# A two-headed SSM kernel with x's first blocks loaded first, more of B turned on TensorE, transfers issued by ScalarE too, and a new order table

## The chip, the cores and the metric

The kernel runs on one core of one Trainium2 chip. The metric is the device time of one launch, in microseconds (us). Three runs of the kernel before took 195.96, 197.85 and 198.28 us, median 197.85 us. In the profile the engines are PE (TensorE; its weight loads are the row PEld), DVE (VectorE), ACT (ScalarE), POOL (GpSimd) and SP (SyncE, which here only issues DMA transfers). A name such as SPq or ACTq is an engine's own queue of instructions.

## What is computed

Two sequence mixers over S = 2048 steps and D = 640 channels, whose results are put side by side. The first (A) is a complex diagonal recurrence, the second (B) a causal convolution of each channel with a filter of 2048 taps, of a product whose one factor is k filtered by four taps.

```python
# A: h[t] = Lam_bar*h[t-1] + B_bar x[t];  y = 2 Re(C h) + x*Dskip
Lam_bar = jnp.exp(dt * Lam);  B_bar = ((Lam_bar - 1.0) / Lam)[:, None] * Bmat
Bu = jnp.einsum("bld,pd->blp", x + 0j, B_bar)
for t in range(L):
    h = Lam_bar[None, :] * h + Bu[:, t, :]
y = 2.0 * jnp.einsum("blp,dp->bld", hseq, Cmat).real + x * Dskip[None, None, :]

# B: kv = (4-tap filter of k) * v;  y = causal convolution of kv with ssm_k, by FFT
k_shift = k_shift + k_pad[:, t:t + S, :] * shift_k[:, ks - 1 - t][None, None, :]
kv = k_shift * v
y_f = rfft(kv_pad) * rfft(kf_pad);  y = irfft(y_f)[:S] + kv * ssm_D
out = concatenate([a, q * y], axis=-1)          # 1 x 2048 x 1280, bfloat16
```

## The kernel before

Everything on chip lies in one SBUF tile, `arena` (columns of bfloat16, given out by name: A the states, BT the turned B, XT the turned x, KT and VT the turned k and v, T scratch, AS and Y the spectra), and one PSUM tile, `acc`, of eight banks. So the profile's names of operands say little, and a step is known by its line.

**Part A.** x comes turned (channels on the partitions) by eight transposing DMAs `load_x` (L525), each with 256 steps, block 7 with the last phases first; B comes turned by transposing DMAs too (L493), but for its rows 0 to 127, which ScalarE's queue fetches plain (L489) and TensorE turns (`turn_B`, L502; eviction L504). Steps are handled by their phase modulo 16, 128 steps of one phase being one column block of A: `base` (L559) multiplies x with B for one state block j of ten; `up2`, `up1` and `up0` sum phases pairwise on the way up, with the powers of Lam_bar as matrices RR (L580); `coarse` runs the recurrence over the 128 chunks on DVE (L654 to L665, with a scan at L659); `down` brings the result back to all phases (L684; an eviction that adds on DVE, L702, or, when ScalarE evicts, an extra matmul with the identity, L682, ahead of it); `project` (L719) multiplies the states of one phase by C, DVE adds x times Dskip to it (L721, after L711 made that product on DVE or POOL), and a DMA stores the rows.

**Part B.** For each of five channel blocks d, k and v come turned (L774), the four taps are multiplied (`cm`, L198 on DVE, L199 on ScalarE), added (`ca`, L800) and multiplied by v (`cx`, L801), and the plane goes to DRAM (L807) and back with the steps split 32 x 64 (`relay`, L817). In two halves hf of 320 channels follow a two-stage forward transform on TensorE of kv and of the filter (`s1`, in a wide form L836 of 16 matmuls of 128 columns, or a narrow one, L841, of 32 matmuls of 64; eviction L846; `s2`, L860, eviction L873), the complex product of the two spectra (`product`: pp L884, pq L887, py L889, pz L891, on DVE or POOL), the inverse (`r2`, L905, eviction L910; `r1`, L926, eviction L938, which multiplies with q) and the store (L950). `load_h` (L767) fetches the filter, and `addD` (L769) adds ssm_D to its first tap ahead of `s1` of the filter.

**What sets the order.** The program adds operations with the engines that may run them, and a table `ORDER` of some 790 entries, one per operation, gives the order in which they are issued, the engine (T, V, A, G, S for PE, DVE, ACT, POOL, SP; a small t is a narrow `s1`) and the PSUM bank. Every engine runs its own instructions in that order, one after the other, and an instruction that waits holds up all behind it on its engine. Waits follow from the footprints of the operands in the arena. An operation's cost in the code, such as `PPOOL: 4.5`, is only what the order was once planned with.

Of the kernel before, what the change touches and what calls it, by code (L numbers as in the profile page):

```python
# [12 lines left out]
bf16 = mybir.dt.bfloat16  # L13
# [170 lines left out]
for _name, _n in (("A", 10 * 16 * 130), ("BT", 6400), ("RR", 5120), ("W", 4096), ("G", 8192), ("XT", 10240), ("AS", 10240),  # L184
                  ("Y", 10240), ("T", 6656), ("KT", 2064), ("VT", 6144), ("H0", 5120), ("KV", 5120), ("YS", 2560), ("I3", 192),
                  ("E", 64), ("JS", 128), ("F1", 256), ("IDF", 192), ("DR", 640), ("SK", 20), ("DM", 160),
                  ("PV", 60), ("SMALL", 1400)):
    LAY.part(_name, _n)
# [149 lines left out]
def params(c):  # L338
# [7 lines left out]
    for k, src in enumerate((lam_re, lam_im, ldt_in)):  # L346
        rows = pr[10 * k:10 * k + 10, :]
        P.add("ld_par", {PSP: .1, PACT: .1}, lambda e, rows=rows, src=src: e.dma_start(
# [3 lines left out]
    P.add("ld_Dr", {PSP: .1}, lambda e: e.dma_start(out=c.DR, in_=bass.AP(dsk_in.tensor, 0, [[0, 128], [1, 640]])), outs=[c.DR],  # L352
# [112 lines left out]
class PartA:  # L465
    def __init__(self, c):
        self.c = c
        v = c.v
        self.A = v("A").rearrange("p (j i s) -> p j i s", j=10, i=16)
        self.BT = []  # L470
        for n, lo in ((2, 0), (4, 1280), (4, 3840)):
# [6 lines left out]
        self.XP = v("XT").rearrange("p (g d s a) -> p d g a s", d=5, g=8, a=2)  # L478
# [3 lines left out]
    def load_B(self, k):  # L482
        c, P = self.c, self.c.P
        n, lo, row = ((2, 0, 0), (4, 1280, 128), (4, 3840, 384))[k]
        raw = c.v("T", 1280, 1280)
        for ri, src in ((0, c.ins["A_B_re"]), (1, c.ins["A_B_im"])):
            if k == 0:
                dst = raw[:, 640 * ri:640 * ri + 640]
                P.add("ld_Braw", {PACT: .1}, lambda e, dst=dst, src=src: e.dma_start(out=dst, in_=src[0:128, :]), outs=[dst], nbytes=128 * 1280)  # L489
                continue  # L490
            dst = c.v("BT", lo + 320 * n * ri, 320 * n).rearrange("p (d m) -> p d m", d=5)
            s = src[row:row + 64 * n, :].rearrange("p (d q) -> p d q", q=128)
            P.add(f"ld_B{k}", {PSP: 64 * n * .0055}, lambda e, dst=dst, s=s: e.dma_start_transpose(out=dst, in_=s), outs=[dst],  # L493
                  nbytes=64 * n * 1280)
        if k == 0:
            idn = c.I3[:, 0:128]
            for r in range(2):
                g, out, part = P.group(1), c.v("BT", 640 * r, 640), raw[:, 640 * r:640 * r + 640]

                def mm(e, B, part=part):  # L500
                    for d in range(5):
                        e.transpose(out=B.bitcast(bf16)[:, 128 * d:128 * d + 128], in_=part[:, 128 * d:128 * d + 128], identity=idn)  # L502
                P.add("turn_B", {PPE: .29}, mm, ins=[part, idn], group=g, nmm=5)
                P.add("ev_B", {PDVE: .5, PACT: .7}, lambda e, B, out=out: c.CP[e](out=out, in_=B.bitcast(bf16)[:, 0:640]), outs=[out], group=g)  # L504
# [51 lines left out]
    def base(self, e, o, j, q):  # L556
        for d in range(5):
            for r in range(2):
                e.matmul(o[64 * r:64 * r + 64], lhsT=self.BT[j][:, r, d, :], rhs=self.XP[:, d, 2 * q:2 * q + 2], start=(d == 0),  # L559
                         stop=(d == 4), skip_group_check=True, tile_position=(0, 64 * r))  # L560

    def base_in(self, j, q):
        return [self.BT[j], self.c.v("XT", 2560 * q, 2560)]

    def up2(self, j0, q):

        c, P = self.c, self.c.P
        g = P.group(2)

        def mm(e, B):  # L570
            for a in range(2):
                self.base(e, B[:, 512 * a:512 * a + 512], j0 + a, 2 + q)
        P.add(f"up2{q}_{j0}", {PPE: 10 * .216}, mm, ins=self.base_in(j0, 2 + q) + [self.BT[j0 + 1]], group=g, nmm=20)
# [596 lines left out]
```

## Time and profile before

The profiled execution has a span of 199.3 us, 1.45 us above the median of the runs.

| engine | busy us | share of the span | instructions |
|---|---|---|---|
| PE | 181.9 | 91% | 3324 |
| DVE | 163.0 | 82% | 225 |
| ACT | 135.8 | 68% | 166 |
| POOL | 73.1 | 37% | 62 |

The page cuts the span into 40 slices and shows in each the busy tenths of an engine. Read from left to right, POOL works in the first quarter (the tables of angles), then now and then; DVE is near full from the second slice on:

```profile
PE   4979999999799999888959988999999999999992
DVE  4705699599868979999898878989989999997941
ACT  3279988959888689998967889983877290192000
POOL 8399800590060050007270385299250004500050
```

PE is at work in nearly every slice, from about 12 us to the end.

### The profile page before, as it was taken

The numbers are of one execution on the slowest core, as the hardware profiler recorded it, in microseconds if no ns is written. First come the engines' busy times: TensorE is split into PE (matmuls) and PEld (weight loads), VectorE is DVE, ScalarE is ACT, GpSimd is POOL, SyncE is SP. The second block draws the span as 40 slices with busy tenths as digits, with TensorE's granted clock in tenths as the row PEclk, the third lists the DMA queues.
The fourth block names the chain that finished last, engine by engine and source line by source line (L and its number), as shares of the span: only waits on it lengthen the run. The fifth ranks groups of instructions, "written<-read, shape, count | busy, mean of one in ns | idle before, by whom it ended". The sixth has DMA issues, their size and how long they took to land.

```text
span 199.3 us, 7475 instructions
## 1 busy us (share of the span) xinstructions
PE 181.9 (91%) x3324; PEld 123.4 (62%) x3324; DVE 163.0 (82%) x225; ACT 135.8 (68%) x166; POOL 73.1 (37%) x62
## 2 busy tenths in 40 slices
PE   4979999999799999888959988999999999999992
PEld 1545555654468674665738654755767786797771
DVE  4705699599868979999898878989989999997941
ACT  3279988959888689998967889983877290192000
POOL 8399800590060050007270385299250004500050
PEclk9999999999999999999997999999999999999999
DMA  5999999999999999999892799028546732375785
GB/s 107 183 174 134 193 134 163 167 155 178 235 221 288 153 169 157 173 138 116 143 286 55 172 134 138 5 79 125 130 127 140 168 99 72 102 199 135 162 200 139
DMA packets 107738, 30.15 MB, mean 151 GB/s; under 512 B 102586, under 2 KB 107066, under 8 KB 107706
## 3 DMA queue, kind: packets, MB, share of 16 engines
q1 hardware_dynamic: 107418, 29.35, 84.0%
q8 instruction: 26, 0.43, 1.0%
q10 hardware_dynamic: 288, 0.33, 0.6%
q14 instruction: 6, 0.05, 0.1%
HBM read 10.99 MB, written 7.86 MB: 95 GB/s over the span
## 4 chain that ended last, share of the span: by engine, by line
PE 52%; DMA 14%; DVE 11%; ACT 11%; SPq 7%; issue 3%; ACTq 0%; DVEq 0%
PE acc L559 18%; PE acc L719 16%; ACT arena L873 6%; DMA arena<-in_A_x_dram 5%; PE acc L860 4%; PE acc L905 4%; SPq L767 4%; DMA arena<-in_B_k_dram 3%; DMA kv_rows<-arena 2%; ACT arena L846 2%; DMA arena<-in_A_B_re_dram 2%; PE acc L684 2%; PE acc L580 2%; DVE arena L721 2%; PE acc L926 2%
## 5 line engine op out<-in xcount | busy, mean ns | idle before, releaser
L559 PE MATMUL acc<-arena 128*64 128x512 bf16 x400 | 47.3, 389 | 1.5 <-DMA arena<-in_A_B_re_dram 1.1
L719 PE MATMUL acc<-arena 128*128 128x320 bf16 x320 | 45.7, 299 | 0.8 <-ACT arena L846 0.6
L873 ACT CAST arena<-acc 128x960 bf16<-128x960 f32 (+1 forms) x41 | 36.2, 916 | 9.2 <-PE acc L860 7.3
L719 PEld LDWEIGHTS <-arena 128*128 128x128 bf16 x320 | 30.3, 98 | 13.4 <-ACT arena L846 0.8
L559 PEld LDWEIGHTS <-arena 128*64 128x64 bf16 x400 | 24.4, 108 | 21.2 <-issue 2.6
L846 ACT CAST arena<-acc 128x1024 bf16<-128x1024 f32 x29 | 27.7, 1054 | 3.0 <-PE acc L836 2.3
L910 ACT CAST arena<-acc 128x1024 bf16<-128x1024 f32 x17 | 16.2, 1035 | 16.4 <-PE acc L905 16.4
L860 PE MATMUL acc<-arena 128*64 128x160 bf16 x512 | 23.7, 238 | 1.4 <-ACT arena L873 0.8
L887 POOL TENSOR_TENSOR arena<-arena 128x1280 bf16<-128x1280 bf16 x6 | 16.7, 2790 | 20.7 <-DVE arena L884 20.7
L860 PEld LDWEIGHTS <-arena 128*64 128x64 bf16 x512 | 18.3, 111 | 9.2 <-ACT arena L873 3.6
L702 DVE TENSOR_TENSOR arena<-acc,arena 128x1024 bf16<-128x1024 f32 (+1 forms) x15 | 17.2, 1166 | 2.4 <-PE acc L684 2.0
L836 PE MATMUL acc<-arena 128*64 128x128 bf16 x400 | 15.2, 227 | 4.3 <-DVE arena L721 2.1
L721 DVE TENSOR_TENSOR arena<-acc,arena 128x640 bf16<-128x640 f32 x16 | 13.2, 823 | 6.8 <-PE acc L719 5.7
L800 DVE TENSOR_TENSOR arena<-arena 128x2048 bf16<-128x2048 bf16 x14 | 17.1, 1220 | 1.0 <-ACT arena L199 0.8
L836 PEld LDWEIGHTS <-arena 128*64 128x64 bf16 x400 | 12.9, 115 | 6.6 <-DVE arena L721 2.2
L846 DVE CAST arena<-acc 128x1024 bf16<-128x1024 f32 x11 | 13.1, 1219 | 4.5 <-PE acc L836 3.9
L889 POOL TENSOR_TENSOR arena<-arena 128x1280 bf16<-128x1280 bf16 x3 | 7.8, 2609 | 19.6 <-DVE arena L887 19.5
L684 PE MATMUL acc<-arena 128*128 128x512 bf16 (+2 forms) x50 | 12.4, 337 | 0.8 <-ACT arena L873 0.7
L199 ACT ACTIVATE arena<-arena 128x2048 bf16<-128x2048 bf16 (+2 forms) x10 | 11.0, 1110 | 2.7 <-DMA arena<-in_B_k_dram 2.7
L884 DVE TENSOR_TENSOR arena<-arena 128x2560 bf16<-128x2560 bf16 x8 | 11.9, 1489 | 0.5 <-ACT arena L873 0.3
L711 POOL TENSOR_TENSOR arena<-arena 128x640 bf16<-128x640 bf16 x4 | 5.8, 1458 | 17.5 <-DMA arena<-in_A_x_dram 17.5
L576 DVE CAST arena<-acc 128x1024 bf16<-128x1024 f32 x4 | 4.9, 1225 | 8.8 <-PE acc L559 8.8
(143 smaller groups left out, 283.4 us busy)
## 6 DMA issues: line engine op xcount, KB each, us to landing
out_dram<-arena SPq DMA_DIRECT2D x32, 160.0 KB, 2.9
arena<-in_B_ssm_k_dram SPq DMA_DIRECT2D x8, 320.0 KB, 7.1
kv_rows<-arena SPq DMA_DIRECT2D x5, 512.0 KB, 4.0
arena<-kv_rows SPq DMA_DIRECT2D x16, 160.0 KB, 5.0
arena<-in_A_x_dram SPq DMA_DIRECT2D x16, 160.0 KB, 3.5
arena<-in_B_q_dram SPq DMA_DIRECT2D x8, 320.0 KB, 4.6
arena<-in_A_B_im_dram ACTq DMA_DIRECT2D x1, 160.0 KB, 2.5
arena<-in_A_B_re_dram ACTq DMA_DIRECT2D x1, 160.0 KB, 2.7
```

What stands on the lines that cost most here:

```text
L559: e.matmul(o[64 * r:64 * r + 64], lhsT=self.BT[j][:, r, d, :], rhs=self.XP[:, d, 2 * q:2 * q + 2], start=(d == 0), stop=(d == 4), skip_gro ...
L684: e.matmul(B[:, o:o + 128 * k], lhsT=c.RR[:, n, j, :], rhs=A[:, j, q:q + k, 0:128], start=not by_pe, stop=True, skip_group_check=True)
L702: e.tensor_tensor(out=o, in0=b, in1=o, op=ALU.add)
L719: e.matmul(B[:, 512 * b:512 * b + 320], lhsT=lh[j], rhs=self.CT[:, j, 320 * b:320 * b + 320], start=(j == 0), stop=(j == 9))
L721: P.add(f"ev_C{i}", {PDVE: dve(640)}, lambda e, B: e.tensor_tensor(out=ys.rearrange("p (b n) -> p b n", b=2), in0=B.rearrange("p (b n) -> ...
L800: P.add(f"ca{d}_{j}", tt, lambda e: e.tensor_tensor(out=t1, in0=t1, in1=t2, op=ALU.add), outs=[t1], ins=[t1, t2])
L836: e.matmul(B[64 * b:64 * b + 64, 128 * i:128 * i + 128], lhsT=lh[i], rhs=F[:, b, :], start=True, stop=True, tile_position=(0, 64 * b))
L846: P.add(f"e1{what}{hf}_{u}", {PACT: act(1024), PDVE: dve(1024)}, lambda e, B: c.CP[e](out=out, in_=(B.rearrange("p (l n s k) -> p k s l n" ...
L860: e.matmul(B[64 * s:64 * s + 64, 512 * b + 160 * i:512 * b + 160 * i + 160], lhsT=c.W[:, k, 64 * b:64 * b + 64], rhs=self.AS[hf][:, k, 160 ...
L873: c.CP[e](out=out, in_=b.rearrange("p r (k j n) -> p r k j n", k=n, j=4) if nj > 1 else b.rearrange("p r (k x) -> p r k x", k=n))
L887: P.add(f"pq{hf}", n2, lambda e, a=a, b=b: e.tensor_tensor(out=X[:, :, a], in0=X[:, :, a], in1=Yk[:, :, b], op=ALU.mult), outs=[X[:, :, a] ...
L910: P.add(f"er2{hf}_{u}", {PACT: act(1024), PDVE: dve(1024)}, lambda e, B: c.CP[e](out=out, in_=B.rearrange("p (s n b) -> p b s n", s=2, n=4 ...
```

## The change

- **Start.** The SP queue begins with x's blocks 7, 6, 5 and 4; B comes transposed only in its rows 384 to 639. Rows 0 to 383 come plain on ScalarE's queue in six transfers and are turned on TensorE in six groups of five (two groups before). There are 3 groups of warming matmuls in place of 6. The parameters, the taps, ssm_D and four of the filter's transfers are issued by ScalarE.
- **Layout.** A holds the states of two successive phases interleaved, `[j][g of 8][258]` in place of `[j][16][130]`, as x lies in XT. `base` so reads x contiguously, and `up0`'s last two steps, the last step of `down` (down3), the result of `coarse` and the weights of `project` are read or written with a stride of two. `up0b` is 256 columns wide with three terms and `up0c` keeps one. `up2` of the last blocks of x is split for j below 6, so that block 7 is used first.
- **Transfers.** ScalarE may issue ld_r, st_A, ld_q, pl, rl, st_B and the small loads. SP's operations fall from 118 to 73, ScalarE's transfers rise from 2 to 33.
- **Order and engines.** The table is new. Of the 40 `s1` groups 38 are narrow (15 before). All adds of `down` are on DVE. POOL may multiply taps, and its operations rise from 58 to 81: 7 tap products (none before), 4 adds `ca` and 2 products `cx` (one `ca` before), 4 spreads of L436 (one before), 16 of the product's parts pq, py and pz (11 before) and 8 products L711 (4 before). DVE has 11 of L800, 3 of L801, 13 of L198, 1 of L436, 16 of L887 to L891 together and 8 of L711 (before: 14, 5, 15, 4, 21 and 12).

```diff
-for _name, _n in (("A", 10 * 16 * 130), ("BT", 6400), ...
+for _name, _n in (("A", 10 * 8 * 258), ("BT", 6400), ...
...
-            P.add(f"ld_B{k}", {PSP: 64 * n * .0055}, lambda e, dst=dst, s=s: e.dma_start_transpose(out=dst, in_=s), outs=[dst],
...
+        if k == 3:
+            for ri, src in srcs:
+                dst = c.v("BT", 3840 + 1280 * ri, 1280).rearrange("p (d m) -> p d m", d=5)
+                s = src[384:640, :].rearrange("p (d q) -> p d q", q=128)
+                P.add(f"ld_B{k}", {PSP: 1.4}, lambda e, dst=dst, s=s: e.dma_start_transpose(out=dst, in_=s), outs=[dst], nbytes=256 * 1280)
+            return
+        raw, idn = c.v("T", 1280 + 1280 * k, 1280), c.I3[:, 0:128]
+        for ri, src in srcs:
+            dst = raw[:, 640 * ri:640 * ri + 640]
+            P.add(f"ld_Braw{k}", {PACT: .1}, lambda e, dst=dst, src=src: e.dma_start(out=dst, in_=src[128 * k:128 * k + 128, :]), outs=[dst],
+                  nbytes=128 * 1280)
...
-                e.matmul(o[64 * r:64 * r + 64], lhsT=self.BT[j][:, r, d, :], rhs=self.XP[:, d, 2 * q:2 * q + 2], start=(d == 0),
+                e.matmul(o[64 * r:64 * r + 64], lhsT=self.BT[j][:, r, d, :], rhs=self.XP[:, d, lo:lo + n], start=(d == 0),
...
-        part(f"up0b_{j0}", 0, 128, ((0, 14), (1, 6), (2, 2)), False, A[:, j0:j0 + 2, 1, 0:128], None)
-        part(f"up0c_{j0}", 128, 128, ((0, 15), (1, 7), (2, 3), (3, 1)), False, self.V[:, j0:j0 + 2, :], None)
+        part(f"up0b_{j0}", w, 256, ((0, 7, w), (1, 3, w), (2, 1, w)), False, A[:, j0:j0 + 2, 0, odd], (slice(0, 256, 2), 256))
+        part(f"up0c_{j0}", first, 128, ((3, 0, odd),), False, self.V[:, j0:j0 + 2, :], (first, 256))
...
-        H = self.A[:, 5 * h:5 * h + 5, 0, 1:129]
+        H = self.A[:, 5 * h:5 * h + 5, 0, 2:258:2]
...
-        lo = 1 if i == 0 else 0
-        lh = [A[:, j, i, lo:lo + 128] for j in range(10)]
+        lo = (2 if i == 0 else 1) if i < 2 else i % 2
+        lh = [A[:, j, i // 2, lo:lo + 255:2] for j in range(10)]
...
-        P.add(f"st_A{i}", {PSP: .5}, lambda e: e.dma_start(out=dst, in_=ys), ins=[ys], nbytes=128 * 1280)
+        P.add(f"st_A{i}", {PSP: .5, PACT: .45}, lambda e: e.dma_start(out=dst, in_=ys), ins=[ys], nbytes=128 * 1280)
...
-            P.add(f"cm{d}_{j}", {PDVE: .7, PACT: act(2048)}, lambda e: c.SM[e](out, k, w), outs=[out], ins=[k, w])
+            P.add(f"cm{d}_{j}", {PDVE: .7, PACT: act(2048), PPOOL: 1.95}, lambda e: c.SM[e](out, k, w), outs=[out], ins=[k, w])
...
-            a.up2(j, q)
+            a.up2(j, q, ((1, 1), (0, 1)) if q and j < 6 else ((0, 2),))
...
-    "140S0 141G0 147A0 75V0 76S0 77S0 8G0 146A0 7G0 9V0 13G0 59G0 0V0 3T1 5T4 21V0 110V0 14V0 18V0 57V0 4T4 15V0 16V0 100G0 19V0 "
+    "10G0 12V0 16V0 30V0 97G0 0V0 1T0 23G0 3T1 144A0 2T0 155A0 98G0 142G0 132G0 68G0 4G0 11V0 15V0 5G0 56G0 138G0 19G0 131G0 "
```

In the changed file most lines stand one earlier (L800 is L799, L801 is L800, L769 is L768, L711 is L710, L887 is L886), while the taps keep L198 and L199.

POOL's queue in the middle of the program, before: the last of the tables (L330) and one spread (L436), then one add of the convolution (L800), the addition of ssm_D for the second half of the filter (L769), and at once the first half's product (L887) and x times Dskip (L711).

```order
L641 COPY arena<-arena 128x1280
L330 TENSOR_TENSOR arena<-arena 128x1024
L436 TENSOR_TENSOR arena<-arena 128x1280
L800 TENSOR_TENSOR arena<-arena 128x2048
L769 TENSOR_TENSOR arena<-arena 128x80
L887 TENSOR_TENSOR arena<-arena 128x8x160
L711 TENSOR_TENSOR arena<-arena 128x640
```

And now, at the same place: L198 is a tap product, L799 an add, L800 the product with v, L768 the addition of ssm_D and L886 the first half's product.

```order
L800 TENSOR_TENSOR arena<-arena 128x2048
L198 TENSOR_SCALAR arena<-arena 128x2048
L799 TENSOR_TENSOR arena<-arena 128x2048
L198 TENSOR_SCALAR arena<-arena 128x2048
L799 TENSOR_TENSOR arena<-arena 128x2048
L198 TENSOR_SCALAR arena<-arena 128x2048
L799 TENSOR_TENSOR arena<-arena 128x2048
L800 TENSOR_TENSOR arena<-arena 128x2048
L198 TENSOR_SCALAR arena<-arena 128x2048 x2
L799 TENSOR_TENSOR arena<-arena 128x2048
L198 TENSOR_SCALAR arena<-arena 128x2048
L768 TENSOR_TENSOR arena<-arena 128x80
```

Block 3 of the convolution, its product and that of block 2, and part of block 4 are now on POOL, 12 operations in a row, and the addition of ssm_D stands behind them.

The start of SP's queue before, with the small loads (L750, L348), x (L525), B (L493) and k (L774):

```order
L750 DMA arena<-in_B_shift_k_dram 128x5x4
L348 DMA arena<-in_A_Lambda_re_dram 10x2x64
L348 DMA arena<-in_A_Lambda_im_dram 10x2x64
L348 DMA arena<-in_A_log_dt_dram 10x2x64
L525 DMA_TRANSPOSE arena<-in_A_x_dram 128x5x256 x2
L493 DMA_TRANSPOSE arena<-in_A_B_im_dram 128x5x256
L493 DMA_TRANSPOSE arena<-in_A_B_re_dram 128x5x256
L525 DMA_TRANSPOSE arena<-in_A_x_dram 128x5x256 x2
L774 DMA_TRANSPOSE arena<-in_B_k_dram 128x2048
```

And now (L524 is x, L489 is B, L773 is k and v):

```order
L524 DMA_TRANSPOSE arena<-in_A_x_dram 128x5x256 x4
L489 DMA_TRANSPOSE arena<-in_A_B_im_dram 128x5x256
L489 DMA_TRANSPOSE arena<-in_A_B_re_dram 128x5x256
L773 DMA_TRANSPOSE arena<-in_B_k_dram 128x2048
L524 DMA_TRANSPOSE arena<-in_A_x_dram 128x5x256 x2
L773 DMA_TRANSPOSE arena<-in_B_v_dram 128x2048
```

The four small loads and one pair of B's transposes went from ahead of k's first block; four blocks of x stand ahead of everything.

More of the change, by code (lines that the diff above doesn't have):

```diff
@@ L495, in load_B @@
[L495 to L504, printed above, removed]
+        srcs = ((0, c.ins["A_B_re"]), (1, c.ins["A_B_im"]))
@@ L606, in up0, with part @@
         js = (j0, j0 + 1)
-        def part(name, lo, n, terms, base, out, dst):
+        first, odd = slice(1, 256, 2), slice(1, 257, 2)
+        def part(name, cols, n, terms, base, out, src):
             def mm(e, B):
```

140 lines of the change are left out of this document (69 added, 71 removed), and 74 rows, old and new, of the table ORDER.

## The prediction

> **What bounds the kernel now.** I read the page's busy times first, then its chain, then PE's timeline for the places at which PE waits.
>
> ```profile
> span 199.3 us, 7475 instructions
> PE 181.9 (91%) x3324; PEld 123.4 (62%) x3324; DVE 163.0 (82%) x225; ACT 135.8 (68%) x166; POOL 73.1 (37%) x62
> PE 52%; DMA 14%; DVE 11%; ACT 11%; SPq 7%; issue 3%; ACTq 0%; DVEq 0%
> ```
>
> ```profile
> 12.52 22.88 PE L559 MATMUL acc<-arena 128*64 128x512 bf16 x200 [1.14 <-DMA arena<-in_A_B_re_dram]
> ...
> 103.24 0.70 PE L836 MATMUL acc<-arena 128*64 128x128 bf16 x16 [2.06 <-DVE arena L721]
> ...
> 172.96 4.14 PE L905 MATMUL acc<-arena 64*128 64x128 bf16 x112
> ```
>
> PE is busy for 181.9 of 199.3 us, so 17.4 us are idle, and the largest single wait that I found behind the start is the 2.06 us at 103.24. The kernel is bound by PE, with DVE close behind; POOL seems to have 126 us to spare, and that is where the change puts work. The question is whether that room is real. The timelines of POOL and DVE answer it (start, duration):
>
> ```profile
> 90.94 4.07 POOL L800 TENSOR_TENSOR arena<-arena 128x2048 bf16<-128x2048 bf16 x1 [17.94 <-DVE arena L198]
> ...
> 99.29 2.61 POOL L887 TENSOR_TENSOR arena<-arena 128x1280 bf16<-128x1280 bf16 x1
> ...
> 113.04 3.06 POOL L887 TENSOR_TENSOR arena<-arena 128x1280 bf16<-128x1280 bf16 x1 [9.54 <-DVE arena L884]
> ```
>
> ```profile
> 90.78 1.22 DVE L702 TENSOR_TENSOR arena<-acc,arena 128x1024 bf16<-128x1024 f32 x1
> ...
> 99.72 2.53 DVE L711 TENSOR_TENSOR arena<-arena 128x640 bf16<-128x640 bf16 x1 [0.63 <-DMA arena<-in_A_x_dram]
> ...
> 112.81 0.82 DVE L887 TENSOR_TENSOR arena<-arena 128x1280 bf16<-128x1280 bf16 x1
> ```
>
> At 99.72 DVE starts x times Dskip while POOL is in a product from 99.29 to 101.90. It ends at 102.25, that is 0.35 us behind POOL's end, and takes 2.53 us for work that otherwise takes 0.48 (below). At 113.04 it is the other way round: DVE is in a product until 113.63, and POOL's takes 3.06 us in place of 2.61, longer by 0.45. So two instructions that both read their operands from SBUF do not run side by side; the later one waits for the whole of the earlier. At 90.78 an addition that reads PSUM takes its full 1.22 us beside POOL's 4.07: with one operand in PSUM, DVE is free. And the wait of 2.05 us at 99.72 is the very one that reached PE at 103.24. POOL's room is therefore only the time in which DVE evicts PSUM or idles, and the two engines' SBUF work adds up as if on one engine. The groups show how much that is (count, then busy us, mean ns):
>
> ```profile
> L887 POOL TENSOR_TENSOR arena<-arena 128x1280 bf16<-128x1280 bf16 x6 | 16.7, 2790 | 20.7 <-DVE arena L884 20.7
> L889 POOL TENSOR_TENSOR arena<-arena 128x1280 bf16<-128x1280 bf16 x3 | 7.8, 2609 | 19.6 <-DVE arena L887 19.5
> L330 POOL TENSOR_TENSOR arena<-arena 128x1024 int32<-128x1024 int32 x4 | 7.6, 1894 | 0.0
> L291 POOL TENSOR_TENSOR arena<-arena 128x1024 int32<-128x1024 int32 x4 | 7.6, 1892 | 0.0
> L711 POOL TENSOR_TENSOR arena<-arena 128x640 bf16<-128x640 bf16 x4 | 5.8, 1458 | 17.5 <-DMA arena<-in_A_x_dram 17.5
> L891 POOL TENSOR_TENSOR arena<-arena 128x1280 bf16<-128x1280 bf16 x2 | 5.2, 2611 | 0.0
> L800 POOL TENSOR_TENSOR arena<-arena 128x2048 bf16<-128x2048 bf16 x1 | 4.1, 4070 | 17.9 <-DVE arena L198 17.9
> L436 POOL TENSOR_TENSOR arena<-arena 128x1280 bf16<-128x1280 bf16 x1 | 2.5, 2517 | 12.0 <-ACT arena L199 12.0
> L641 POOL COPY arena<-arena 128x1280 f32<-128x1280 f32 x1 | 1.3, 1251 | 10.7 <-PE acc L836 10.7
> ```
>
> ```profile
> L800 DVE TENSOR_TENSOR arena<-arena 128x2048 bf16<-128x2048 bf16 x14 | 17.1, 1220 | 1.0 <-ACT arena L199 0.8
> L884 DVE TENSOR_TENSOR arena<-arena 128x2560 bf16<-128x2560 bf16 x8 | 11.9, 1489 | 0.5 <-ACT arena L873 0.3
> L198 DVE TENSOR_SCALAR arena<-arena 128x2048 bf16<-128x2048 bf16 x15 | 11.0, 749 | 0.2
> L801 DVE TENSOR_TENSOR arena<-arena 128x2048 bf16<-128x2048 bf16 x5 | 8.1, 1624 | 0.1
> L887 DVE TENSOR_TENSOR arena<-arena 128x1280 bf16<-128x1280 bf16 x10 | 8.1, 820 | 0.1
> L711 DVE TENSOR_TENSOR arena<-arena 128x640 bf16<-128x640 bf16 x12 | 7.8, 654 | 1.0 <-DMA arena<-in_A_x_dram 1.0
> L436 DVE TENSOR_TENSOR arena<-arena 128x1280 bf16<-128x1280 bf16 x4 | 5.9, 1484 | 0.0
> L891 DVE TENSOR_TENSOR arena<-arena 128x1280 bf16<-128x1280 bf16 x6 | 5.1, 846 | 0.2
> L889 DVE TENSOR_TENSOR arena<-arena 128x1280 bf16<-128x1280 bf16 x5 | 4.1, 818 | 0.0
> L659 DVE TENSOR_TENSOR_SCAN arena<-arena 128x640 bf16<-128x640 f32 x2 | 3.0, 1487 | 0.0
> ```
>
> With the waits taken out (L887 on POOL at L889's 2.61; L801 at the 1.22 of the equal L800; L711 on DVE without the one of 2.53, (7.8 - 2.53)/11 = 0.48 each), POOL's rows give 57.6 us and DVE's 78.0, together **135.6 us** of SBUF work. All but the last two of POOL's L711 (2.9 us) stands ahead of the first inverse transform of the second half, so 132.7 us. That transform is the row at 172.96: 40 us of those 173 are short operations of the setup, and time in which neither engine had SBUF work. From 172.96 to the span's end are 26.3 us of PE work and the last stores.
>
> **The change part by part.**
>
> *Work moved to POOL.* Each move costs POOL more than DVE saves. Five of L800 and L801: 5 x 4.07 = 20.4 added on POOL, 5 x 1.22 = 6.1 saved on DVE. Five parts of the product: 13.1 against 4.1. Three spreads of L436: 7.6 against 4.4. Four products L711: 5.8 against 1.9. Seven tap products: no row has one on POOL. The nearest is the one-operand copy L641, 1.25 us for 1280 elements, so 2.0 for 2048; the ends are 1.25 each and the two-operand 4.07, or 8.8 to 28.5 for the seven; I take 14.0, by the copy's rate. DVE gives up two taps, 1.5 (the others come from ScalarE). Added 60.9, saved 18.0: the SBUF work of both goes from 135.6 to **178.5 us**. Five L711 on POOL stand at its end; without their 7.1 us, 171.4 us have to be done before the second half's first inverse transform.
>
> Whether a tap on POOL excludes DVE too, no long row shows; if none did, 14 us of this would not add. [...]
>
> *How late the transform is then.* With no idle time but the first 12.5 us (the row at 12.52: only setup runs until there), it starts at 12.5 + 171.4 = 183.9 us. With all of the 40.2 us of before, at 211.6. When the port is the bound, something nearly always waits for it, but both engines are in order, and each waits for loads and for PE; I take a little over half, 22 us: 193.4, and with 26.3 behind it 219.7.
>
> *Who waits on the way.* On POOL the addition of ssm_D, which `s1` of the second filter half needs, now stands behind a run of six two-operand instructions and six taps, 6 x 4.07 + 6 x 2.0 = 36.4 us; behind it are the first half's products, for which the inverse transform waits. DVE's own additions of the taps and the short steps of the coarse scan, each after the other, meet a POOL instruction of 2 to 4 us at nearly every step, and its evictions, for which PE waits, queue behind them.
>
> *Gains.*
>
> ```profile
> L836 PE MATMUL acc<-arena 128*64 128x128 bf16 x400 | 15.2, 227 | 4.3 <-DVE arena L721 2.1 <-ACT arena L600 1.2 <-ACT arena L846 0.7
> ...
> L841 PE MATMUL acc<-arena 64*64 64x64 bf16 x480 | 6.1, 195 | 0.9 <-ACT arena L846 0.6 <-ACT arena L600 0.2
> ...
> L719 PEld LDWEIGHTS <-arena 128*128 128x128 bf16 x320 | 30.3, 98 | 13.4 <-ACT arena L846 0.8 <-DVE arena L873 0.3 <-DVE arena L938 0.3
> ...
> L905 PEld LDWEIGHTS <-arena 64*128 64x128 bf16 x320 | 10.7, 145 | 1.2 <-ACT arena L910 0.3 <-issue 0.3 <-DVE arena L721 0.2
> ```
>
> A wide `s1` group (16 matmuls) takes 15.2/25 = 0.61 us, a narrow one (32) 6.1/15 = 0.41; 23 groups turn narrow, which saves PE 4.6. Weights read with a stride of two in `project` have no row; the dearest loads are L905's, and at 145 in place of 98 ns the 320 would cost 15.0 more, beside PE's matmuls (123.4 us of PEld beside 181.9), so I cost them at nothing; a gain is not in it, since they were contiguous. The start, from the chain (start, duration):
>
> ```profile
> 2.51 1.45 SPq L525
> ...
> 5.74 1.77 SPq L493
> ...
> 7.56 4.82 DMA arena<-in_A_B_re_dram
> ```
>
> x's transposes went out at 2.51 and can now at 0.7, 1.8 us sooner; the transposed B, issued at 5.74 and landed at 12.38, no longer holds PE. If x's block 7 ends its issue at 2.2 and lands 4.8 later, at 7.0, base can run from 7.0 and not from 12.52 with 2.46 us of it done (an estimate): 3.1 us gained. Both gains are PE's, 7.7 us. In the forecast they vanish, since PE then waits for DVE and POOL.
>
> *Transfers on ScalarE.*
>
> ```profile
> 1.19 0.46 ACTq L489 DMA_DIRECT2D arena<-in_A_B_re_dram  x1
> ```
>
> At 0.46 us, 31 more issues are 14.3 us on ScalarE; at the 1.45 of an SP issue above they would be 45. Against it five taps leave it. With 135.8 busy it has room for the first and hardly for the second; I take 14.3 hidden in that room, so nothing on the path; if all came between evictions that PE waits for, it would be 14.3.
>
> **The rivals.**
>
> *Faster.* POOL's SBUF work falls mostly into DVE's evictions and idle time, which the row at 90.78 shows to be possible; then PE stays the bound and keeps its gains: 199.3 - 7.7 = 191.6 in the profile, 190 by the runs. It decides where DVE's SBUF work and POOL's together leave PE its due times, which the 2.05 us wait speaks against: already at 135.6 us they collide. Chance 0.12.
>
> *No change.* The lock costs some, the gains repay it, or ScalarE's issues eat them: 199.3 - 7.7 + about 7 = 198.6, 197 by the runs. Chance 0.06.
>
> *Slower by less.* Only the run ahead of the addition of ssm_D hurts. Were it to start at 80 us, eleven before POOL's L800 does now, it ends at 116.4, and the product behind it, at 99.29 now, is 17.1 late; less the gains of 7.7 and an estimated 2 that PE finds to do meanwhile, 199.3 + 17.1 - 9.7 = 206.7, 205 by the runs. Chance 0.17.
>
> **The numbers.** The profiled execution is 1.45 us above the median of 197.85, so the forecast of 219.7 is **218 us**, chance 0.65. Its own ends are the two starts above, 210.2 and 237.9 with 26.3 behind, less 1.45: 209 and 236; with taps that do not add, 218 - 14 = 204. The range 204 to 236 holds forecast and milder case. A measurement of this kernel tells 2% from no change, 194 to 202: faster 0.12, same 0.06, slower 0.82.
>
> **What would show it.** In the new profile DVE's L800 and products should have means well above 1.22 and 0.82 us, POOL be busy for some 130 us, and PE show waits of several us released by DVE or POOL, the largest ahead of the second filter half's `s1` and of the inverse transforms; L905 of the second half should start near 193. DVE means near those of before, with POOL's rows lying under PSUM evictions, would prove it wrong, as would a narrow `s1` group of 0.6 us or a base that starts at 12 the gains.

## The result: 273.7 us in place of 197.85

The changed kernel takes 273.7 us (272.27 to 277.26, five runs), 1.388 times the time before (95% interval 1.376 to 1.401): slower, as forecast, but by 76 us and not by 20, and outside the range of 204 to 236. One count in the section on the change and in the prediction was wrong too: ScalarE issues 49 transfers now, not 33; 43 of them were SP's before and six are B's plain rows. The two profiles are of executions slower than most (the fast runs' spans are 193 to 197 us before and 270 to 273 after), and every time below is a median of fast runs, set against fast runs of the kernel before beside it.

The page after, its span, busy times and chain:

```profile
span 275.1 us, 8246 instructions
PE 195.3 (71%) x3688; PEld 133.0 (48%) x3692; DVE 218.6 (79%) x227; ACT 123.9 (45%) x147; POOL 168.3 (61%) x85
DVE 24%; PE 22%; issue 8%; DMA 8%; ACT 1%; SPq 0%; DVEq 0%; ACTq 0%
```

PE was the bound with 91% of the span; now it is idle for 80 us, and the chain, which the page follows back for 63% of the span, runs through DVE more than through PE. POOL's 73 us became 168, and DVE's 163 became 219 although DVE was given less SBUF work (it took over some evictions). PE's timeline (start, duration, the wait ahead of it) has the three places that correspond to the rows shown of before: the start of base, the first inverse transform of the second half, and the end.

```profile
23.53 2.35 PE L558 MATMUL acc<-arena 128*64 128x256 bf16 x20 [10.39 <-ACT arena L503]
...
236.51 5.34 PE L904 MATMUL acc<-arena 64*128 64x128 bf16 x96 [7.62 <-DVE arena L720]
...
257.26 4.45 PE L718 MATMUL acc<-arena 128*128 128x320 bf16 x16 [2.87 <-issue]
```

Base starts at 23.53 (the main run at 12.52 before), after a wait of 10.4 us for ScalarE; the inverse transform starts at 236.5 (forecast 193.4, before 172.96). The groups of DVE and POOL that the forecast rested on (count, busy us, mean ns):

```profile
L198 POOL TENSOR_SCALAR arena<-arena 128x2048 bf16<-128x2048 bf16 x7 | 38.7, 5527 | 0.4
...
L701 DVE TENSOR_TENSOR arena<-acc,arena 128x1024 bf16<-128x1024 f32 x16 | 19.2, 1218 | 2.3 <-ACT arena L845 1.0 <-PE acc L682 0.6 <-ACT arena L872 0.5
L799 DVE TENSOR_TENSOR arena<-arena 128x2048 bf16<-128x2048 bf16 x11 | 18.1, 1646 | 0.2
...
L799 POOL TENSOR_TENSOR arena<-arena 128x2048 bf16<-128x2048 bf16 x4 | 17.3, 4334 | 0.9 <-DVE arena L198 0.7
...
L886 DVE TENSOR_TENSOR arena<-arena 128x1280 bf16<-128x1280 bf16 x10 | 15.9, 1606 | 0.3
...
L656 DVE TENSOR_TENSOR_SCAN arena<-arena 128x640 bf16<-128x640 f32 x2 | 6.4, 3189 | 0.1
```

A tap on POOL takes 5.53 us, where I had taken 2.0; on DVE it was 0.75. DVE's adds went from 1.22 to 1.65 us, its products from 0.82 to 1.61, the scan from 1.49 to 3.19: the waits that the forecast looked for are there. The additions of `down`, which read one operand from PSUM, kept their time (L701, 1.22 us before and after). And a wait that the forecast had costed at nothing is at the very start. ScalarE's timeline:

```profile
3.55 0.41 ACTq L494 DMA_DIRECT2D arena<-in_A_B_im_dram  x1
11.26 0.55 ACTq L348 DMA_DIRECT2D arena<-in_A_Lambda_re_dram  x1
12.77 0.29 ACTq L348 DMA_DIRECT2D arena<-in_A_log_dt_dram  x1
14.83 0.59 ACTq L754 DMA_DIRECT2D arena<-in_B_ssm_D_dram  x1
16.46 0.29 ACTq L348 DMA_DIRECT2D arena<-in_A_Lambda_im_dram  x1
18.55 0.43 ACTq L749 DMA_DIRECT2D arena<-in_B_shift_k_dram  x1
21.14 0.32 ACTq L766 DMA_DIRECT2D arena<-in_B_ssm_k_dram  x1
21.49 1.28 ACT L503 ACT_TABLE_LOAD   x1 [21.49 <-DMA arena<-in_B_shift_k_dram]
22.78 1.29 ACT L503 COPY arena<-acc 128x640 bf16<-128x640 bf16 x2
```

The issues themselves take 0.3 to 0.6 us, but between them ScalarE stands, from 3.96 to 21.1 us, and B's eviction, for which PE waits, is queued behind. What it waits for, this program shows: each of its transfers is given one of eight completion counters, whichever engine issues it, and an issue waits until the earlier transfer on that counter is complete. The head of ScalarE's queue with its waits:

```
L348 DMA arena<-in_A_Lambda_re_dram 10x2x64 [waits DMAHW6_49,DVE_49]
L348 DMA arena<-in_A_log_dt_dram 10x2x64 [waits DMAHW7_49]
L754 DMA arena<-in_B_ssm_D_dram 4x80 [waits DMAHW1_49,Pool_49]
L348 DMA arena<-in_A_Lambda_im_dram 10x2x64 [waits DMAHW2_49]
```

The issues follow the landings: the fifth of ScalarE's own plain loads of B, on counter 6, has landed at 11.18, and Lambda_re goes out at 11.26; SP's third transpose of x, on counter 7, has landed at 12.74, and log_dt goes out at 12.77. So a small load on ScalarE stands behind plain rows of B and behind the long transposes of x, B and k on SP's queue.

### The profile page after: what moved, and what is told of

It reads as the page before. It is cut to its first block, busy times and chain, and to the rows that moved or that the text cites. A ratio compares the mean times of both kernels' runs of the same rounds, so it can differ in the third digit from the quotient of the medians.

```text
span 275.1 us, 8246 instructions
## 1 busy us (share of the span) xinstructions
PE 195.3 (71%) x3688; PEld 133.0 (48%) x3692; DVE 218.6 (79%) x227; ACT 123.9 (45%) x147; POOL 168.3 (61%) x85
## 4 chain that ended last, share of the span: by engine, by line
DVE 24%; PE 22%; issue 8%; DMA 8%; ACT 1%; SPq 0%; DVEq 0%; ACTq 0%
PE acc L718 9%; DMA arena<-in_A_x_dram 7%; DVE arena L886 4%; PE acc L682 3%; PE acc L904 3%; DVE arena L662 3%; DVE arena L720 3%; DVE arena L883 3%; PE acc L925 2%; DVE arena L710 2%; DVE arena L656 2%; PE acc L840 2%; DVE arena L198 2%; DVE arena L872 1%; PE acc L859 1%
## 5 line engine op out<-in xcount | busy, mean ns | idle before, releaser
L558 PE MATMUL acc<-arena 128*64 128x512 bf16 (+1 forms) x460 | 50.5, 378 | 15.9 <-ACT arena L503 10.4
L872 ACT CAST arena<-acc 128x960 bf16<-128x960 f32 (+1 forms) x33 | 29.4, 916 | 22.7 <-PE acc L859 21.6
L198 POOL TENSOR_SCALAR arena<-arena 128x2048 bf16<-128x2048 bf16 x7 | 38.7, 5527 | 0.4
L840 PE MATMUL acc<-arena 64*64 64x64 bf16 x1216 | 16.5, 204 | 17.8 <-issue 6.2
L710 POOL TENSOR_TENSOR arena<-arena 128x640 bf16<-128x640 bf16 x8 | 13.4, 1682 | 24.7 <-DMA arena<-in_A_x_dram 24.7
L886 POOL TENSOR_TENSOR arena<-arena 128x1280 bf16<-128x1280 bf16 x6 | 15.9, 2648 | 20.2 <-DVE arena L883 20.2
L840 PEld LDWEIGHTS <-arena 64*64 64x64 bf16 x1216 | 13.7, 116 | 25.6 <-issue 11.3
L701 DVE TENSOR_TENSOR arena<-acc,arena 128x1024 bf16<-128x1024 f32 (+2 forms) x19 | 21.4, 1140 | 2.9 <-PE acc L682 1.2
L198 DVE TENSOR_SCALAR arena<-arena 128x2048 bf16<-128x2048 bf16 (+2 forms) x16 | 19.5, 1239 | 0.6 <-DMA arena<-in_B_k_dram 0.4
L904 PE MATMUL acc<-arena 64*128 64x128 bf16 x320 | 13.6, 250 | 8.8 <-DVE arena L720 8.8
L890 POOL TENSOR_TENSOR arena<-arena 128x1280 bf16<-128x1280 bf16 x6 | 18.0, 3001 | 2.5 <-DVE arena L886 1.6
L937 DVE TENSOR_TENSOR arena<-acc,arena 128x960 bf16<-128x960 f32 (+1 forms) x12 | 12.0, 1041 | 8.2 <-PE acc L925 8.2
L799 DVE TENSOR_TENSOR arena<-arena 128x2048 bf16<-128x2048 bf16 x11 | 18.1, 1646 | 0.2
L799 POOL TENSOR_TENSOR arena<-arena 128x2048 bf16<-128x2048 bf16 x4 | 17.3, 4334 | 0.9 <-DVE arena L198 0.7
L682 PE MATMUL acc<-arena 128*128 128x512 bf16 (+2 forms) x50 | 13.9, 379 | 5.4 <-DVE arena L662 5.0
```

The source lines that it names most:

```text
L198: vm = lambda e: lambda out, in_, by: e.tensor_scalar_mul(out=out, in0=in_, scalar1=by)
L682: e.matmul(B[:, o], lhsT=c.RR[:, n, j, :], rhs=fr(j, q, k), start=not by_pe, stop=True, skip_group_check=True)
L701: e.tensor_tensor(out=o, in0=b, in1=o, op=ALU.add)
L799: P.add(f"ca{d}_{j}", tt, lambda e: e.tensor_tensor(out=t1, in0=t1, in1=t2, op=ALU.add), outs=[t1], ins=[t1, t2])
L840: e.matmul(B[64 * b:64 * b + 64, 512 * l + 64 * i:512 * l + 64 * i + 64], lhsT=lh[i][ps], rhs=F[ps, b, 64 * l:64 * l + 64], start=True, st ...
L872: c.CP[e](out=out, in_=b.rearrange("p r (k j n) -> p r k j n", k=n, j=4) if nj > 1 else b.rearrange("p r (k x) -> p r k x", k=n))
```

## The experiments

Three theories: **P**, POOL's SBUF work costs DVE its time (what the prediction and the expectations call the port or the lock; the rows show one engine waiting for the other, 2.53 us in place of 0.48 at 99.72 of before, and no port); **S**, ScalarE stands at its transfers; **O**, the new order is slow whoever does the work. Edits are to the order table, where an entry is the operation's number, its engine and its bank. Times are medians; the kernel before, run beside them, took 195.3 to 198.5 us, and a cost is the difference from the one beside it.

### Taking parts of the change back, in its own order

Seven taps from POOL to DVE:

```diff
-372G0 438G0 440G0 442G0 448G0 449G0 451G0
+372V0 438V0 440V0 442V0 448V0 449V0 451V0
```

> The changed kernel with its seven tap products moved from POOL back to DVE, at the same places of the order. The changed kernel takes 273.7 us. Theory P (POOL's SBUF work adds to DVE's, and a tap on POOL takes 5.53 us where I had put 2.0): 38.7 us leave POOL, 7 x 0.75 = 5.3 come to DVE, so about 33 us less, near 240 us. Theory S (ScalarE, standing at its transfers, is what costs): 5 us less at most. Theory O (the new order is slow by itself, whoever does the work): 5 us less at most.

Measured 271.99 us: next to nothing gained. By itself this would have overturned theory P. But PE has a wait in this run that the changed kernel has not, of 25 us, and DVE says why. PE's timeline, then DVE's list of waits (us in total, times, longest):

```profile
143.55 0.75 PE L548 MATMUL acc<-arena 64*64 64x320 bf16 x8 [25.12 <-DVE arena L701]
```

```profile
DVE arena L198 <- POOL arena L799: 12.5, 3, 4.2
...
DVE arena L198 <- POOL arena L800: 8.3, 1, 8.3
```

The adds are still on POOL, so the taps, in one queue before, now go to and fro: DVE stands 20.8 us at a tap whose scratch a POOL add or product is still reading, and the additions of `down` (L701), which PE needs, stand behind. All 24 operations back on DVE:

> The changed kernel with all 24 operations that came to POOL moved back to DVE at the same places of the order: seven taps, five adds and products of the convolution, three spreads, five parts of the product, four x times Dskip. Theory P: 38.7 + 20.4 + 7.6 + 13.1 + 5.8 = 85.6 us leave POOL and about 24 come to DVE, so 55 to 60 us less, 214 to 219 us. Theory S: 10 us less at most. Theory O: 250 us or more stay.

265.85 us, 8 less. ScalarE's transfers, but for B's, on SP (43 entries, such as):

```diff
-73A0 75A0 139A0 74A0 137A0 172A0
+73S0 75S0 139S0 74S0 137S0 172S0
```

> The changed kernel with all of ScalarE's transfers but the six of B issued by SP, at the same places of the order. Theory S: the 10.4 us that PE waits at the start for an eviction of ScalarE go, and of the 25 us that ScalarE stands ahead of its transfers in all most go too: 250 to 262 us. Theory P: 0 to 5 us less, since DVE and POOL are the bound behind the start. Theory O: no change.

257.87 us, 16 less: base now starts at 9.09 us. Both together:

> Both edits at once: POOL's 24 operations back on DVE and ScalarE's transfers but for B's back on SP; the new layout, start, narrow s1 and order stay. Theories P and S together account for the loss if this comes to 195 to 205 us. Theory O: 215 us or more stay, and the order itself has to be looked at.

253.07 us. And every operation on the engine that it had before, still in the new order:

> The changed kernel in its own order, but every operation that exists in both on the engine that it had before: POOL's 24 and ScalarE's transfers back, and the evictions, taps and parts of products too. Theory E (it is the sharing out among engines: DVE at 84% of the span with ScalarE at 49% when only POOL's and the transfers were put back): 200 to 220 us. Theory O (the sequence itself, with its late loads of k and its queues that wait for one another): 240 us or more.

296.95 us, 23 more. Read alone, these five speak for theory O: with every engine's work as before, the new program in its new sequence takes 101 us more than the kernel before, and 85 more than the same program in the old sequence (below). But a sequence is made for its engines. In e4_both PE waits for DVE's additions of `down`:

```profile
121.08 0.75 PE L548 MATMUL acc<-arena 64*64 64x320 bf16 x8 [15.27 <-DVE arena L701]
```

Ahead of them DVE does taps, adds and a product that POOL had done, some 7 us, then stands 1.9 us for a load of k that the sequence asks for late and 4.2 for the one add left on POOL. An edit taken back inside a sequence made around it leaves its place in every queue, and puts a new wait there. So I asked the other way round.

### Putting parts of the change into the old order

The whole new program, with new layout and start, in the old order with the old engines. B's loads, turns and evictions are set in by hand:

```diff
-147A0
+144A0 149A0 150A0 155A0 156A0
...
-146A0
+143A0
...
+151T3 153T4 157T5 159T6 152V3 154A4 158V5 160A6
```

> The changed program (new layout, B's rows 0 to 383 turned on TensorE, 256-column up0b) emitted in the order of the kernel before, with that kernel's engines, banks, transfers on SP and 15 narrow s1; only the loads, turns and evictions of B are set in by hand. Theory O (the new order, with its engines, costs nearly all): 192 to 199 us, beside 198 for the kernel before. Theory L (reading with a stride of two, or B's turning, costs): 205 us or more.

211.65 us, 1.076 times the kernel before (interval 1.054 to 1.097). That is 15 us, in the range named for theory L; but of L's two halves it isn't the stride that shows. The loads and matmuls of `project`, with weights read at a stride of two, are what they were (98 and 299 ns before):

```profile
L718 PE MATMUL acc<-arena 128*128 128x320 bf16 x320 | 45.9, 300 | 2.0 <-issue 1.3 <-ACT arena L845 0.6
...
L718 PEld LDWEIGHTS <-arena 128*128 128x128 bf16 x320 | 30.3, 98 | 14.8 <-issue 1.5 <-ACT arena L845 0.8 <-DVE arena L872 0.3
```

The loss begins at the start, with B's turning, in PE's timeline of this run:

```profile
9.05 1.25 PE L501 MATMUL acc<-arena 128*128 128x128 bf16 x10 [4.02 <-DMA arena<-in_A_B_re_dram]
...
12.95 17.53 PE L558 MATMUL acc<-arena 128*64 128x256 bf16 x220
```

B's first turn waits 4.0 us for a plain load, and base starts at 12.95; before, one group ran from 8.92. From there the delay grows to 9 us by the coarse scan, through waits for evictions, and stays. Part of it is of my making: of the two loads that the first turn needs (143 and 144), the second was set in as the last of the six. In e3_act, with the new order's start, base runs from 9.09. So part of these 15 us need not be the change's own; how much isn't shown. Issuing the other four loads later, to let the first two land sooner:

> The changed program in the old order (211.7 us), with B's rows 128 to 383 issued by ScalarE behind its first table load and turned behind the first group of base. If the start was late because six plain loads and x's transposes share the transfer engines (PE waited 4.0 us for the first of them): 204 to 208 us. If the 13 us lie elsewhere: 210 to 213 us.

219.99 us, worse, and for theory S's reason: the first turn now runs at 5.22 us, but ScalarE stands at the four loads until 14.5, and PE for its eviction.

```profile
16.11 3.86 PE L558 MATMUL acc<-arena 128*64 128x256 bf16 x40 [7.96 <-ACT arena L503]
```

What the new start is worth when it is set in well was not tried in the old order.

Twelve operations of the convolution on POOL, in the kernel before:

```diff
-362A0 390V0 428V0 429V0 430V0 431V0 432V0 433V0 434V0 438V0 439V0 441V0
+362G0 390G0 428G0 429G0 430G0 431G0 432G0 433G0 434G0 438G0 439G0 441G0
```

> The kernel before with seven taps and five adds and products of its convolution on POOL, the same as in the changed kernel, at their old places in the order. Theory P (POOL's SBUF work costs DVE its time): 7 x 5.4 + 5 x 4.07 = 58 us on POOL for 7 x 0.75 + 5 x 1.22 = 11 on DVE, in a chain that DVE and PE wait for: 215 us or more. Rival (POOL's work is hidden, as putting the taps back suggested): 198 to 203 us.

235.48 us, 40 more, as theory P expects. The taps alone:

> The kernel before with only the seven taps on POOL, the five adds and products staying on DVE. If each tap on POOL takes 5.4 us and slows or blocks DVE like the adds: 38 of the 58 us that b1_conv put on POOL, so two thirds of its 37 us: 220 to 228 us. If a one-operand tap leaves DVE mostly free: 200 to 210 us, and the adds are the cost.

227.38 us, 31 of the 40. That a tap on POOL does keep DVE waiting is seen here (POOL, then DVE):

```profile
104.92 10.87 POOL L198 TENSOR_SCALAR arena<-arena 128x2048 bf16<-128x2048 bf16 x2 [4.30 <-DMA arena<-in_B_k_dram]
```

```profile
105.72 3.98 DVE L801 TENSOR_TENSOR arena<-arena 128x2048 bf16<-128x2048 bf16 x1
```

A product of 1.22 us takes 3.98. And the queue behind costs as well: DVE's list of waits in this run has

```profile
DVE arena L800 <- POOL arena L198: 16.3, 3, 10.4
```

16.3 us in which DVE stands at an add for a tap that POOL hasn't done. DVE itself is busy for 173.4 us here, 10.4 more than before, though six taps (4.5 us) left it, so some 15 us are waits inside its instructions. Of the 31 us about half would therefore come from POOL being slow in a chain that DVE waits for, even if the two shared nothing; the page's chain of b4_taps runs through POOL for 24% of the span, that of b1_conv for 32%. Theory P's adding up of SBUF work is only the other half, and no run separates the two by itself. The run of POOL ahead of the addition of ssm_D, my third rival, makes PE wait 10.0 us in b1_conv. With that addition on DVE:

> b1_conv (235.5 us) with the addition of ssm_D for the second filter half on DVE in place of POOL, so that it no longer stands behind POOL's run. If the 10 us that PE waited for it were on the path: 224 to 227 us. If DVE and POOL were late there anyway: 232 to 236 us.

240.45 us, 5 more, outside both ranges: its operands come late as well, and now DVE stands 10.1 us for their transfer. So the wait was seen, but not on the path by itself. The other half of POOL's moves (spreads, products, x times Dskip):

> The kernel before with the other half of POOL's moves: the spreads of L436, the parts of the product and x times Dskip on the engines that the changed kernel has them on (three spreads, five parts and four L711 more on POOL). By the port's sum: 26.5 us more on POOL, 10.4 less on DVE, so 10 to 25 us: 208 to 223 us. If they fall beside evictions: 198 to 203 us.

227.07 us, 30 more, above the end that I had given the sum. Here it is the waits inside DVE's instructions: DVE is busy for 13.9 us more though 10.4 left it, and POOL is 8% of the page's chain. Short steps of the setup now wait for nearly a whole operation of POOL; this one took 0.18 us before:

```profile
31.71 2.61 POOL L436 TENSOR_TENSOR arena<-arena 128x1280 bf16<-128x1280 bf16 x1
```

```profile
32.06 2.30 DVE L415 TENSOR_TENSOR arena<-arena 128x20 f32<-128x20 f32 x1
```

The transfers on ScalarE:

> The kernel before with the same 43 transfers issued by ScalarE, in the old order. Theory S (ScalarE stands at each transfer until what it depends on, and the transfer eight before it, is done, and evictions stand behind): 208 us or more. Rival (an issue costs 0.46 us and no wait): 198 to 203 us.

219.93 us, 24 more: theory S. Of these the eleven small loads of the start:

> The kernel before with only the 11 small loads of the start (parameters, taps, ssm_D, the filter's first four, Dskip) on ScalarE; the other 32 transfers stay on SP. If the 21 us of all 43 come from the start, where PE waited 6 us for a parameter: 212 to 220 us. If they come from the stores and relays later: 199 to 206 us.

204.30 us, 7 of the 24, by the wait for a parameter that b2_act shows too:

```profile
11.41 0.18 PE L356 MATMUL acc<-arena 128*128 128x30 bf16 x1 [6.04 <-DMA arena<-in_A_log_dt_dram]
```

The other 17 are left for the 32 later relays, loads and stores, which were not run by themselves. Then all at once, in the old order: first start, convolution and transfers, then POOL's other twelve as well.

> The changed program in the old order (211.7 us by itself) with the twelve taps, adds and products on POOL (37 us more when put into the kernel before) and the 43 transfers on ScalarE (21 us more). If the three costs are those of the change and add up, whatever the order: 211.7 + 37 + 21.4 = 270 us, the 273.7 of the changed kernel without its order. If they hide one another: 235 to 250 us, and the new order has to have cost the rest. Theory O (the new order by itself loses much): 250 us or less.

> The changed program in the old order with all of POOL's 24 moves and the 43 transfers on ScalarE (h2_all, 261.5 us, with the spreads, products and L711 too). If placing the work on engines, with the start, is the whole loss: 270 to 285 us, as much as the changed kernel's 273.7 in its own order. If these twelve are hidden: 260 to 265 us, and the remaining 10 us are the new order's.

261.54 us, between the ranges named, and 271.7 us. With everything but the new order (and its narrow s1 and evictions) the kernel is as slow as the changed one's 273.7. That is 60 us above h1_oldorder, by moves alone. So the moves are enough for the loss, and on top of them the sequence adds only 2 us. They are not shown to be the only cause: with the old engines the same sequence costs 85 us (e5_engines against h1_oldorder). Each is slow without the other, the two together hardly slower than either, and no run divides the 76 us between them. Since h1_oldorder's 15 us are perhaps partly mine, up to some 17 us may be the new sequence's even in this count.

### Two terms by themselves

All `s1` narrow, in the kernel before (25 entries, such as):

```diff
-184T2 172T0 178T0 188T4
+184t2 172t0 178t0 188t4
```

> The kernel before with all 40 s1 groups narrow (15 before). If the 0.20 us that a narrow group saves PE reaches the end: 25 x 0.20 = 5 us less, 193 to 195 us. Rival (the groups wait for their evictions anyway, or the changed order of rows within a group costs the eviction): 197 to 200 us.

201.81 us, slower by 2.9% (1.8 to 3.9). PE's matmuls of s1 do fall from 15.2 + 6.1 us to 16.7, as expected. But PE's waits ahead of them show something else, waits in which nothing in the trace holds it back:

```profile
PE acc L841 <- issue: 5.5, 5, 1.7
```

A narrow group has twice the matmuls and weight loads (7475 instructions became 8275), and five of them start late by 1.1 us each on average. The profiled span is 198.8 us, against 193.6 to 195.6 of the kernel before beside it. The 5.5 us of waits are of the size that would undo the gain, but why PE starts late there stays open.

Does the exclusion cost in the kernel before as well? Sixteen operations that POOL does behind its tables on DVE, and then the one product whose collision reached PE:

> The kernel before with all that POOL does after its tables on DVE: the one add of the convolution, the spread, the eleven parts of products and the four L711. By the port's sum 34.5 us leave POOL for 13.6 on DVE, 21 us less SBUF work, and no DVE instruction waits for a product: 192 to 196 us, faster than the kernel before. If DVE, 82% busy, is then the bound: 199 to 206 us.

> The kernel before with only POOL's first product (the L887 at 99.29 us, for which DVE's L711 waited 2.05 us and PE after it) on DVE. If that one collision is on the path: 1 to 2 us less, 195 to 197 us. If the 0.8 us that DVE gains in work make up for it: no change.

205.91 us, 4.1% slower (2.8 to 5.4), and 196.9 us, no change (1.001, interval 0.998 to 1.004). In the first run the spread stayed on POOL, and by the prediction's prices the sixteen take 38.6 us there and 12.2 on DVE, not 34.5 and 13.6. So 26 us less SBUF work made the kernel slower: it gains from what POOL does, as it would if these operations lie beside DVE's evictions, which was seen for one of them (the row at 90.94 of before). In the second run PE's wait of 2.05 us is gone and nothing is gained, so the collision from which the forecast began was not on the path.

| edit to the old kernel or order | us | against the kernel before |
|---|---|---|
| convolution's 12 on POOL | 235.5 | +40 |
| of these the 7 taps | 227.4 | +31 |
| the other 12 on POOL | 227.1 | +30 |
| 43 transfers on ScalarE | 219.9 | +24 |
| new layout and start, as set in here | 211.7 | +15 |
| all of these | 271.7 | +75 |
| the change | 273.7 | +76 |

The four single costs (40, 30, 24, 15) add to 109, so they overlap by 34 us where one wait covers another.

## Why the prediction was wrong in size

**Two steps failed: the price of a tap on POOL, a term of the sum, and the transfers on ScalarE, a term put at nothing.** The mechanism stood in part: DVE and POOL do hold each other up (DVE's adds went from 1.22 to 1.65 us, POOL's from 4.07 to 4.33). The forecast was a sum: 171.4 us of SBUF work ahead of the second half's first inverse transform, 22 us of slack, 26.3 us behind it. The trace gives its three terms anew.

- *The price of a tap, a term of the sum.* "I take 14.0, by the copy's rate": the seven took 38.7, 24.7 more. The range named 28.5 as the upper end, by a two-operand row, and the truth is above it. That the taps' time adds to DVE's in full, as the sum has it, no run shows; what the runs showed is a two-operand instruction of DVE let go 1.5 to 1.9 us before the end of a tap of 5.4 to 6.2 (below). b4_taps shows that this term carries: 31 us for the taps alone.
- *The slack.* With the taps at their price, 196.1 us of work stand ahead of the transform at 236.5, so 40.4 us are left over, against the 22 that I took: 18.4 us more. That this is nearly the 40.2 of before is chance. With ScalarE's transfers back on SP (e3_act) and the same work on POOL, the transform starts at 221.52, which leaves 25.4. So most of the 18.4 us is the price of the transfers, and the 22 were near. In the old order it is some 26 (b1_conv, transform at 207.5), 33 (b4_taps, at 200.1) and 52 us (b7_pool12, at 196.7): it differs with what is moved, and that 22 were near here is partly luck.
- *The end.* From the transform to the end of the span 38.6 us, not 26.3. PE is busy in it for 30.3 us (22.7 before), because the new order leaves 208 more matmuls of `r1` behind the transform and because matmuls take longer (those of `project` 327 ns in place of 299, of `r2` 276 in place of 225, of `r1` 215 in place of 199), beside a mean granted clock of 0.83 in this stretch, 1.00 before. Besides, PE idles for some 5 us more, among it 2.87 us at 257.26 and 1.77 us at 248.43 in which it is released by nothing that the trace shows. 12.3 us more.

24.7 + 18.4 + 12.3 = 55.4, which is 275.1 less the 219.7 forecast. That is arithmetic; the causes are those that the runs separate. The other steps of the prediction:

- *"I take 14.3 hidden in that room, so nothing on the path."* Wrong: 24 us (b2_act), and 16 gained when they are taken back (e3_act). I priced the issue at 0.46 us, and the trace bears that out (0.3 to 0.6 in the rows above); what I left out is the wait ahead of the issue. Its rows were there before, in SP's list of waits, 37.9 us ahead of ten stores of A's rows alone (L725). There only transfers stood behind; on ScalarE the evictions wait too. I had also counted 31 more issues where there are 47.
- *The start, "3.1 us gained".* Base was to run from 7.0; where ScalarE doesn't stand at transfers it runs from 9.09 (e3_act), 3.4 us before the 12.52 of the main run, of which 2.46 had been done by then: about 1 us gained. In the change ScalarE's wait turns it into a start at 23.53.
- *Narrow s1, 4.6 us.* The matmul time fell by that much, the kernel's did not (b3_narrow).
- *Strided weights at nothing.* Right: 98 and 300 ns in h1_oldorder.
- *The addition of ssm_D behind POOL's run,* the rival of a smaller loss: in the changed kernel PE waits 0.6 us for it, 10.0 in b1_conv, where moving it doesn't help. It did not decide.
- *Faster,* by POOL's work falling beside evictions: the kernel before gains by what is on POOL (b8_nopool); 24 more operations did not.

The forecast's signs were mostly right: DVE's means above 1.22 and 0.82 us, PE's waits released by DVE, the one ahead of the inverse transform among the largest; the largest of all, 10.4 us at the start, is ScalarE's. POOL's busy time was to be some 130 us and is 168, 25 of the difference being the taps, the rest in the main waits inside its instructions.

## What to carry to other kernels

POOL's idle share, 63% of the span, was not room: twelve more operations on it cost 40 us. So count the stretches in which its work can run beside the neighbour's, and price an operation by a row of the same form on the same engine; where there is none, as for the tap (5.53 us, priced at 2.0), measure one first. Before a transfer is given to an engine that evicts, ask what its issue waits for, not what it takes: SP, which only issues, stood 37.9 us ahead of ten stores in the kernel before, and with 43 transfers on ScalarE, which evicts, the same kernel took 24 us more. And test the parts of a change from both ends, added to the order that it came from and taken out of the order made for it: here the seven taps cost 31 us when added and gave back 2 when taken out, ScalarE's transfers 24 and 16, and neither alone shows how the parts combine.

## What the runs showed of the chip

**A one-operand multiplication on POOL** of 128 x 2048 bfloat16 by a scalar per partition takes 5.44 us, the first one mostly beside evictions, more than the two-operand add of the same size, 4.06. Its hold on DVE has two lengths. POOL's, then DVE's timeline of the changed kernel:

```profile
39.41 5.44 POOL L198 TENSOR_SCALAR arena<-arena 128x2048 bf16<-128x2048 bf16 x1
...
95.39 5.45 POOL L198 TENSOR_SCALAR arena<-arena 128x2048 bf16<-128x2048 bf16 x1
...
105.69 5.55 POOL L198 TENSOR_SCALAR arena<-arena 128x2048 bf16<-128x2048 bf16 x1
```

```profile
42.39 2.48 DVE L412 TENSOR_SCALAR arena<-arena 128x10 f32<-128x10 f32 x1
...
97.57 1.88 DVE L654 TENSOR_TENSOR arena<-arena 128x640 bf16<-128x640 bf16 x1
99.38 2.01 DVE L198 TENSOR_SCALAR arena<-arena 128x2048 bf16<-128x2048 bf16 x1
...
105.97 4.89 DVE L656 TENSOR_TENSOR_SCAN arena<-arena 128x640 bf16<-128x640 f32 x1
110.89 0.49 DVE L659 TENSOR_TENSOR arena<-arena 128x640 bf16<-128x640 bf16 x1
```

DVE's two-operand L654 ends at 99.45, and without its usual 0.49 us it was let go at 98.96, 3.6 us after the tap began and 1.9 before its end at 100.84; the scan, less its 1.49, at 109.4, 3.7 after the tap of 105.69; the product beside a tap in b4_taps, less 1.22, at 108.5, 3.6 after 104.92. Ten such cases stand in the timelines of the changed kernel, b1_conv and b4_taps, and in all of them the two-operand instruction of DVE is let go 1.5 to 1.9 us before the tap's end. The one-operand L412 (less its usual 0.17) and L198 (less 0.75) on DVE are let go only at the tap's end, at 44.7 of 44.85 and 100.6 of 100.84. A two-operand operation of POOL held L655 (103.43 to 105.94, less 0.49) to about its own end at 105.59. So the prediction's "the later one waits for the whole of the earlier" holds beside POOL's two-operand operations, and not quite beside its taps; what makes the two lengths, no run shows.

**The granted clock** was lower where PE idled more: 0.991 in the profile before (17 us idle), 0.983 in h1_oldorder (29), 0.960 in b2_act (33), 0.920 in b1_conv (50), 0.895 after (80); b6_start, with 1.000 at 22 us idle, is an exception. Between executions of one kernel it doesn't follow the time: spans of 270.2 and 273.4 us of the changed kernel had 0.874 and 0.906. With it PE's busy time went from 181.9 to 195.3 us, though the instructions changed too, so that the share of the clock in the loss isn't separated.
